# First loads of a linear-attention block from two issuing engines: tile 1 and the keys' weight on ScalarE, the rest of x on SyncE

## The chip, the cores and the metric

One core of one Trainium2 chip runs the whole program. The metric is the device time of one launch in microseconds. The core's engines are TensorE (PE; PEld are its weight loads), VectorE (DVE), ScalarE (ACT), GpSimd (POOL) and SyncE (SP). Each runs its own instructions in the order in which they were issued, and they wait for each other by semaphores. Sixteen DMA engines move data between HBM and SBUF.

## The reference

A pre-norm transformer block on 2048 tokens of width 512, with linear attention of 32 heads (16 wide) and a ReLU feed-forward of width 1792; all inputs are bf16.

```python
def _A_ref(x, wqkv, wo):
    qkv = (x @ wqkv).reshape(B, S, 3, H, Dh) ...      # q, k, v
    phi = lambda t: jnp.where(t > 0, t + 1, jnp.exp(t)) + 1e-6
    pq, pk = phi(q), phi(k)
    kv = jnp.einsum("bhsd,bhse->bhde", pk, v)
    z = jnp.einsum("bhsd->bhd", pk)
    num = jnp.einsum("bhqd,bhde->bhqe", pq, kv)
    den = jnp.einsum("bhqd,bhd->bhq", pq, z)[..., None] + 1e-6
    return (num / den) ... @ wo
h  = x + _A_ref(_layernorm(x), A_wqkv, A_wo)
h2 = h + relu(_layernorm(h) @ B_w1) @ B_w2
```

## The kernel before, in words

**Tiles.** The 2048 tokens are cut into 16 tiles of 128; tile t holds tokens p * 16 + t for partition p. One tile of x is 128 KB: each partition reads one piece of 1 KB from HBM. A load of n neighbouring tiles reads n KB in one piece per partition. The keys' weight (columns 512 to 1023 of `wqkv`) is 512 KB in `wk_sb`, as four blocks of 128 rows; a half is two blocks, 256 KB, in pieces of 1 KB.

**Order.** There is no loop nest. The string `ORDER` lists every step of the kernel by hand, and the last lines of the function call `op_<name>` for each word with its numbers. Since each engine works in issue order, the string sets each engine's own sequence. The words that matter here:

- `lx.t.n` loads n tiles of x from tile t, and `lk.k.n` loads n blocks of the keys' weight from block k; both are issued by SyncE.
- `table` loads ScalarE's function table; `warm.n.b` are TensorE matmuls on zeros that nothing reads.
- `S.t`, `A.t` (VectorE): statistics and mean/variance of tile t. `R.t.n` (ScalarE): reciprocal standard deviation. `N.t` (VectorE): the normalised tile.
- `T.t.b` (TensorE) and `E.t` (ScalarE): transposed tile through PSUM, for tiles 0 to 3. `X.t` (SyncE): the same for later tiles, by a DMA that transposes.
- `K.t.b.k.n` (TensorE): tile t of the keys, n of the four blocks of the product with `wk_sb`. `K.0.3.0.2` needs only blocks 0 and 1, `K.0.3.2.2` blocks 2 and 3.
- `F`, `U` (ScalarE), `M`, `D` (VectorE): phi of the keys: exp, ReLU, minimum, sum. `D.t` writes the features.
- `G.t` (TensorE): the features of tile t times its normalised tile, summed over the 16 tiles.

The first stretch on VectorE is S.0 S.1 A.0 S.2 A.1 S.3 A.2 N.0 A.3 N.1 N.2 N.3 S.4 S.5 A.4 A.5 S.7 N.5 S.6 M.0 A.7 A.6 D.0. On TensorE it is eleven warm-up matmuls, T.0 to T.3, then K.0 (first half), K.1 (first half), K.0 (second half), K.3, K.2 (first half), K.1 (second half), K.2 (second half), G.0, G.3, K.5, K.4. On SyncE it is ten loads (tiles 0, 1, 2, 3, half 0, tiles 4-5, half 1, tiles 6-7, 8-11, 12-15) and then X.5, X.4. ScalarE begins with the table load, then R.0.

Of the kernel before, what the change touches and what calls it, by code (L numbers as in the profile page):

```python
# [15 lines left out]


ORDER = """
const masks table lx.0.1 lx.1.1 lx.2.1 S.0 S.1 A.0 S.2 warm.1.6 lx.3.1 A.1 R.0.1 S.3 A.2 R.1.1 warm.9.6 N.0 A.3
N.1 R.2.1 R.3.1 lk.0.2 N.2 N.3 warm.1.6 T.0.2 T.1.7 lx.4.2 T.2.5 lk.2.2 S.4 E.0 S.5 T.3.4 A.4 K.0.3.0.2 E.1  # L20
K.1.0.0.2 lx.6.2 E.2 E.3 A.5 R.4.2 K.0.3.2.2 S.7 F.0.1 N.5 S.6 K.3.7 M.0.1 lx.8.4 K.2.2.0.2 U.0.1 lx.12.4 A.7
A.6 K.1.0.2.2 D.0.1 F.3.1 U.3.1 R.6.2 N.4 K.2.2.2.2 M.3.1 G.0 D.3.1 G.3 F.2.1 F.1.1 N.6 N.7 S.8 S.9 X.5 X.4
M.2.1 A.8 A.9 U.2.1 U.1.1 K.5.1 R.8.2 K.4.0 M.1.1 D.2.1 F.4.2 D.1.1 N.9 U.4.2 N.8 X.7 S.12 X.6 X.9 G.2 K.7.3
S.13 A.12 A.13 G.1 K.6.2 K.9.1 M.4.2 S.10 R.12.2 F.6.2 N.12 D.4.2 S.11 A.10 U.6.2 X.8 lq.0.2 M.6.2 N.13 G.4 X.12
K.8.0 A.11 R.10.2 D.6.2 lv.0.2 X.13 G.5 G.6 N.10 N.11 S.15 S.14 F.8.2 M.8.2 U.8.2 G.7 X.11 A.15 A.14 D.8.2
R.14.2 N.15 K.12.0 N.14 za.2 za.4 X.10 G.9 lq.2.2 lv.2.2 K.13.1 K.11.3 F.12.2 U.12.2 X.15 X.14 l2.10.4 l2.3.4
l1.0.2 K.10.2 G.8 M.12.2 F.10.2 U.10.2 za.6 D.12.2 M.10.2 za.8 D.10.2 Q.0.0.0 Q.0.1.1 qF.0.0.2 qU.0.0.2 za.10
qM.0.0.2 K.15.3 G.12 K.14.2 F.14.2 G.11 Q.0.2.0 Q.0.3.1 qF.0.2.2 G.13 za.12 M.14.2 W.14.2 zf.12 qD.0.0.2
qM.0.2.2 qU.0.2.2 G.10 G.14 z.3.3.14 G.15 z.1.3.14 z.2.3.14 z.0.3.14 qD.0.2.2 zc Q.1.0.2 gA.0.2 gA.2.2 zh dn.0.1
Q.1.1.3 dnl.0 kv.0.4 kv.2.4 kv.1.4 kv.3.4 lo.0.2 lo.2.2 dnx.0.2.2 qF.1.0.2 dnx.0.0.2 Q.1.2.0 rt.2.7 kx qM.1.0.2  # L30
Q.1.3.1 qF.1.2.2 m.0.4 m.1.5 rv.2 qW.1.0.2 qM.1.2.2 Q.3.1.7 m.3.6 Q.2.3.2 l1.2.2 dt.3 mA.0.2 qW.1.2.2 dt.0 dt.1
m.2.5 Q.2.1.4 dn.1.3 mA.2.2 dm.0.0.2 dm.0.2.2 dnl.1 dnx.1.2.2 Q.2.2.1 h.3.6 dnx.1.0.2 h.1.5 hD.3 dt.7 qF.2.2.2
rt.6.3 s.3 dt.4 re.6 h.0.0 hD.1 qU.2.2.2 dt.5 a.3 hD.0 s.1 s.0 qM.2.2.2 a.0 Q.3.0.6 h.2.5 Q.2.0.3 n.3 n.0 a.1
dm.1.0.2 Q.3.2.0 Q.3.3.1 dm.1.2.2 x.0 x.3 hD.2 n.1 s.2 qF.3.0.2 qU.2.0.2 qF.2.0.2 h.5.2 h.6.3 a.2 qU.3.0.2
qF.3.2.2 qM.2.0.2 h.4.7 n.2 qD.2.0.2 t.2.5 qD.2.2.2 hD.5 hD.4 h.7.4 dn.2.6 hD.7 e.2 dnl.2 x.1 hD.6 qM.3.0.2
p.0.0.5 dnx.2.2.2 p.0.13.7 p.0.1.6 p.0.8.2 p.0.11.4 qD.3.0.2 s.4 dnx.2.0.2 p.0.9.3 l2.7.3 dt.10 pA.0.0.2 dt.11
l2.0.3 dt.9 dt.8 p.0.12.6 qM.3.2.2 qW.3.2.2 s.6 pD.0.12.2 p.0.3.1 p.0.2.0 pA.0.8.2 s.7 r.0.4 dn.3.6 p.0.5.3
p.0.4.2 a.7 dm.2.0.2 dnl.3 pA.0.2.2 dnx.3.0.2 dnx.3.2.2 pA.0.4.2 dm.2.2.2 p.0.7.7 h.9.0 h.8.5 p.0.6.6 n.7 s.5
dt.13 dt.12 p.0.10.3 hD.9 hD.8 s.8 a.6 pD.0.6.2 dt.15 a.4 n.6 dt.14 pA.0.10.2 f.1.1.0.7 dm.3.0.2 dm.3.2.2 h.11.0
f.1.1.7.7 h.12.4 fo.1 s.9 h.15.6 h.14.5 h.10.3 f.0.2.0.7 a.8 a.9 a.5 hD.11 n.5 hD.12 x.6 hD.15 f.3.4.0.7 h.13.7  # L40
f.3.4.7.7 x.7 s.12 n.8 n.4 hD.14 f.0.2.7.7 x.4 x.5 p.1.0.6 f.2.5.0.7 s.11 s.14 hD.13 fo.3 fo.0 hD.10 a.11 s.10
n.9 p.1.5.3 p.1.1.7 s.15 a.12 pA.1.0.2 p.1.4.2 f.2.5.7.7 p.1.13.7 p.1.3.1 a.10 n.12 r.4.4 pA.1.4.2 p.1.2.0 n.11
p.1.8.4 fo.2 a.14 a.15 s.13 p.1.12.6 n.10 p.1.7.2 pD.1.2.2 n.14 p.1.6.1 x.11 p.1.9.5 pA.1.6.2 x.10 a.13 n.15 x.9
x.8 pD.1.8.2 fd.3 f.5.3.0.7 f.7.0.0.7 p.1.10.1 fd.1 fd.0 pA.1.12.2 p.1.11.2 pA.1.10.2 p.2.9.7 p.2.11.6 f.7.0.7.7
p.2.10.5 p.2.5.1 f.5.3.7.7 fo.7 pD.2.10.2 p.2.8.6 p.2.4.0 r.8.4 f.4.4.0.7 f.4.4.7.7 fo.5 p.2.0.2 pD.2.8.2
pD.2.4.2 p.2.1.3 x.12 n.13 p.2.3.6 p.2.2.5 fd.2 f.6.0.0.7 x.14 x.13 pA.2.0.2 pA.2.2.2 x.15 fo.4 p.3.3.7 p.3.7.1
p.3.2.6 p.3.9.5 p.3.8.4 f.6.0.7.7 pD.3.2.2 fo.6 pD.3.8.2 fd.4 p.3.11.7 p.3.4.2 p.3.10.6 p.3.5.3 p.3.6.0
pA.3.10.2 fd.7 pA.3.6.2 p.2.7.7 fd.5 fd.6 p.2.6.6 pA.2.6.2 p.3.13.5 pD.3.4.2 p.3.0.1 p.3.1.2 p.2.13.7 p.2.12.6
f.11.3.0.7 p.3.12.4 pA.3.0.2 pA.2.12.2 r.12.4 pD.3.12.2 f.9.6.0.7 f.14.2.0.7 f.10.7.0.7 f.11.3.7.7 f.10.7.7.7
f.9.6.7.7 f.8.1.0.7 f.12.5.0.7 f.8.1.7.7 f.13.0.0.7 f.15.4.0.14.3.1 f.14.2.7.7 fo.9 fo.10 fo.11 fd.10 fd.11 fd.9  # L50
f.12.5.7.7 fo.8 f.13.0.7.7 f.15.3.0.14.0.2 fd.8 fo.14 fo.12 fo.13 fo.15.3.1 fd.12 f.15.1.0.14.2.1 fd.13
fd.15.3.1 fd.14 fo.15.0.2 fd.15.0.2 fo.15.2.1 fd.15.2.1
"""
# [3 lines left out]
def kernel(  # L57
# [144 lines left out]

    def load_d(dst, src, k, n):
        nc.sync.dma_start(out=dst[:, k : k + n, :], in_=src[:, k : k + n, :])  # L204
# [376 lines left out]
```

## Time and profile before

| | |
|---|---|
| median of 3 runs | 170.55 us (170.41 to 173.28) |
| the profiled execution | 170.57 us |
| its span, first to last instruction | 168.9 us |
| busy: PE / DVE / ACT / POOL | 96% / 60% / 40% / 3% of the span |
| data moved | 15.49 MB, of which the first ten loads 2.5 MB |
| granted TensorE clock | 1.00 |

In a row of the timeline stand the start and the duration in us, engine and line, what is written and read, the count, and in brackets the idle time before it with what ended that. Neighbouring instructions of one kind are merged into one row with their count. DMA issues are listed on SPq (and would be on ACT's queue) with the time that the issue took; the transfer itself lasts longer, and "us to landing" counts from the issue to its last byte.

### The profile page before, as it was taken

To read this page: it belongs to the slowest core of one execution; us is meant where nothing else is said; L and a number is where in the kernel's file an instruction comes from. 1 tells how busy PE (TensorE), PEld (TensorE's weight loads), DVE (VectorE), ACT (ScalarE), POOL (GpSimd) and SP (SyncE) were. 2 spreads that over 40 slices of the span, in tenths; PEclk is the share of its full clock that TensorE was granted. 3 is DMA by queue.
4 is the path that set the end of the run, shared out by engine and by line. 5 is a ranking of instruction groups with operands and counts; after the bars stand their busy time and mean duration, and the time that the engine had idled before them with its cause. 6 is when DMAs were issued, how large, how long until landed. Compare 5 with 4: busy or idle time off the path is not lost.

```text
span 168.9 us, 2311 instructions
## 1 busy us (share of the span) xinstructions
PE 162.5 (96%) x871; PEld 76.1 (45%) x871; DVE 101.1 (60%) x202; ACT 67.7 (40%) x100; POOL 4.7 (3%) x21
## 2 busy tenths in 40 slices
PE   7779999999999999999999999999999999999993
PEld 2333444445554454544444444444444444444552
DVE  3979999997577999776977372047203600204152
ACT  3886784847879865652000504200220245000000
POOL 7300000000000000000000000000000000000000
DMA  5964485999133363534130116300320000002113
GB/s 124 276 240 92 89 178 117 217 385 336 37 64 62 64 157 67 151 62 97 33 64 0 31 36 157 86 4 0 80 76 0 31 4 0 0 0 88 36 35 93
DMA packets 30635, 15.49 MB, mean 92 GB/s; under 512 B 23200, under 2 KB 29600, under 8 KB 30624
## 3 DMA queue, kind: packets, MB, share of 16 engines
q1 hardware_dynamic: 30624, 15.34, 34.9%
q8 instruction: 7, 0.11, 0.3%
q14 instruction: 4, 0.03, 0.1%
HBM read 7.86 MB, written 2.10 MB: 59 GB/s over the span
## 4 chain that ended last, share of the span: by engine, by line
PE 91%; DMA 3%; SPq 2%; DVE 1%; issue 1%
PE bk L530 29%; PE bk L510 29%; PE bk L351 8%; PE bk L307 8%; PE bk L494 8%; PE bk L299 6%; DMA x_nat<-in_A_x_dram 3%; SPq L201 1%; PE bk L448 1%; PE bk L392 1%; SPq L204 1%; PE bk L404 1%; PE bk L270 0%; DVE st L226 0%; DVE pk_lo L327 0%
## 5 line engine op out<-in xcount | busy, mean ns | idle before, releaser
L530 PE MATMUL bk<-w_sb,at 128*128 128x512 bf16 (+2 forms) x252 | 50.7, 355 | 0.0
L510 PE MATMUL bk<-lnT,w_sb 128*128 128x512 bf16 x224 | 50.5, 379 | 0.0
L516 ACT ACTIVATE at<-bk 128x1024 bf16<-128x1024 f32 x17 | 17.3, 1021 | 55.6 <-PE bk L510 55.6
L530 PEld LDWEIGHTS <-at 128*128 128x128 bf16 x252 | 23.6, 98 | 25.2 <-DVE at L521 0.2
L510 PEld LDWEIGHTS <-w_sb 128*128 128x128 bf16 x224 | 21.8, 98 | 26.0
L538 DVE SCALAR_TENSOR_TENSOR gT<-bk,rstd,h_nat 128x512 bf16<-128x512 f32 (+2 forms) x18 | 12.2, 690 | 31.2 <-PE bk L530 31.2
L521 DVE TENSOR_SCALAR at<-bk 128x1024 bf16<-128x1024 f32 x11 | 13.3, 1220 | 20.7 <-PE bk L510 20.4
L317 ACT ACTIVATE eb<-bk 128x1024 bf16<-128x1024 f32 (+1 forms) x18 | 16.6, 926 | 6.7 <-PE bk L299 4.0
L307 PE MATMUL bk<-lnT,wq_sb 128*128 128x512 bf16 x64 | 15.8, 379 | 0.0
L299 PE MATMUL bk<-wk_sb,lnT 128*128 128x512 bf16 x64 | 15.3, 379 | 0.0
L494 PE MATMUL bk<-m_sb,pqs 128*128 128x512 bf16 x64 | 15.3, 379 | 0.0
L351 PE MATMUL bk<-at,h_nat 128*128 128x512 bf16 x56 | 13.6, 379 | 0.0
L320 ACT ACTIVATE rb<-bk 128x1024 bf16<-128x1024 f32 (+1 forms) x14 | 12.5, 903 | 0.7 <-PE bk L307 0.7
L226 DVE BATCH_NORM_STATS2 st<-x_nat 128x6 f32<-128x512 bf16 x16 | 10.5, 684 | 3.0 <-DMA x_nat<-in_A_x_dram 3.0
L500 DVE TENSOR_TENSOR h_nat<-bk,x_nat 128x512 bf16<-128x512 f32 x16 | 10.6, 681 | 2.4 <-PE bk L494 2.3
L228 DVE BATCH_NORM_STATS2 st<-h_nat 128x6 f32<-128x512 bf16 x16 | 10.8, 685 | 0.1
L351 PEld LDWEIGHTS <-h_nat 128*128 128x128 bf16 x64 | 6.2, 97 | 8.8 <-issue 1.8
L299 PEld LDWEIGHTS <-lnT 128*128 128x128 bf16 x64 | 5.9, 98 | 7.8 <-DMA lnT<-h_nat 1.4
L494 PEld LDWEIGHTS <-pqs 128*128 128x128 bf16 x64 | 6.1, 98 | 7.2 <-DVE pqs L484 0.8
L307 PEld LDWEIGHTS <-wq_sb 128*128 128x128 bf16 x64 | 5.9, 97 | 6.5 <-DMA wq_sb<-in_A_wqkv_dram 0.4
L461 ACT ACTIVATE wk_sb<-ld 128x1024 bf16<-128x1024 f32 x8 | 8.1, 1051 | 0.1
L324 DVE TENSOR_SCALAR eb<-eb 128x1024 bf16<-128x1024 bf16 (+1 forms) x18 | 6.9, 383 | 0.6 <-ACT eb L317 0.6
(61 smaller groups left out, 89.0 us busy)
## 6 DMA issues: line engine op xcount, KB each, us to landing
out_dram<-gT SPq DMA_DIRECT2D x15, 128.0 KB, 1.9
w_sb<-in_B_w_dram SPq DMA_DIRECT2D x2, 896.0 KB, 8.4
x_nat<-in_A_x_dram SPq DMA_DIRECT2D x2, 512.0 KB, 7.0
w_sb<-in_B_w_dram SPq DMA_DIRECT2D x2, 512.0 KB, 4.8
w_sb<-in_B_w_dram SPq DMA_DIRECT2D x2, 384.0 KB, 3.5
x_nat<-in_A_x_dram SPq DMA_DIRECT2D x4, 128.0 KB, 2.5
wk_sb<-in_A_wqkv_dram SPq DMA_DIRECT2D x2, 256.0 KB, 4.2
x_nat<-in_A_x_dram SPq DMA_DIRECT2D x2, 256.0 KB, 5.0
```

What stands on the lines that cost most here:

```text
L228: op_s = lambda t: nc.vector.bn_stats(out=st2[:, t, :], in_=h_nat[:, t, :])
L299: nc.tensor.matmul(bk[:, b, :], lhsT=lnT[c][:, kd, j * P : (j + 1) * P], rhs=wk_sb[:, kd, :], start=(kd == 0), stop=(kd == KD - 1),)
L307: nc.tensor.matmul(bk[:, b, :], lhsT=wq_sb[:, kd, j * P : (j + 1) * P], rhs=lnT[c][:, kd, :], start=(kd == 0), stop=(kd == KD - 1),)
L317: nc.scalar.activation(out=buf(eb, kind, i, n), in_=bank(at_bank[kind, i], n), func=ACT.Exp)
L320: nc.scalar.activation(out=buf(rb, kind, i, n), in_=bank(at_bank[kind, i], n), func=ACT.Relu)
L351: nc.tensor.matmul(bk[:, KD + kd, :], lhsT=ln_nat[:, t, kd * P : (kd + 1) * P], rhs=pk(t)[:, 0, :], start=(t == 0), stop=(t == NT - 1),)
L494: nc.tensor.matmul(bk[:, b, :], lhsT=pqs[:, (c * KD + jb) % NQ, j * P : (j + 1) * P], rhs=m_sb[:, jb, :], start=(jb == 0), stop=(jb == KD ...
L510: nc.tensor.matmul(bk[:, b, cols], lhsT=w1_sb[:, kd, f * P : (f + 1) * P], rhs=lnT[c][:, kd, cols], start=(kd == 0), stop=(kd == KD - 1),)
L516: nc.scalar.activation(out=acts[c % 2][:, f : f + n, :], in_=bank(at_bank["p", c, f], n), func=ACT.Relu)
L521: nc.vector.tensor_scalar(out=acts[c % 2][:, f : f + n, :], in0=bank(at_bank["p", c, f], n), scalar1=0.0, scalar2=None, op0=ALU.max,)
L530: nc.tensor.matmul(bk[:, b, 0 : w * P], lhsT=acts[c % 2][:, f, j * P : (j + 1) * P], rhs=w2_sb[:, f, k * P : (k + w) * P], start=(f == 0), ...
L538: nc.vector.scalar_tensor_tensor(out=o_t[:, t % NO, cols], in0=bk[:, at_bank["f", t, k], 0 : w * P], scalar=rstd2[:, t : t + 1], in1=h_nat ...
```

## The change

Two steps are added, `xa` and `la`, which issue the loads of x and of the keys' weight from ScalarE. `xa.1.1 la.0.2 la.2.2` come ahead of `table` in the order, so they are ScalarE's first three instructions. SyncE issues tile 0, tiles 2 and 3 in one transfer, 4-5, 6-7, 8-11 and 12-15, all ahead of the first S. The words `lx.1.1`, `lx.2.1`, `lx.3.1`, `lk.0.2` and `lk.2.2` are gone, and the later `lx` words are moved forward. All other words stand in the old sequence, though the lines of the string break elsewhere.

```diff
 ORDER = """
-const masks table lx.0.1 lx.1.1 lx.2.1 S.0 S.1 A.0 S.2 warm.1.6 lx.3.1 A.1 R.0.1 S.3 A.2 R.1.1 warm.9.6 N.0 A.3
-N.1 R.2.1 R.3.1 lk.0.2 N.2 N.3 warm.1.6 T.0.2 T.1.7 lx.4.2 T.2.5 lk.2.2 S.4 E.0 S.5 T.3.4 A.4 K.0.3.0.2 E.1
-K.1.0.0.2 lx.6.2 E.2 E.3 A.5 R.4.2 K.0.3.2.2 S.7 F.0.1 N.5 S.6 K.3.7 M.0.1 lx.8.4 K.2.2.0.2 U.0.1 lx.12.4 A.7
...
+const masks xa.1.1 la.0.2 la.2.2 table lx.0.1 lx.2.2 lx.4.2 lx.6.2 lx.8.4 lx.12.4 S.0 S.1 A.0 S.2 warm.1.6 A.1
+R.0.1 S.3 A.2 R.1.1 warm.9.6 N.0 A.3 N.1 R.2.1 R.3.1 N.2 N.3 warm.1.6 T.0.2 T.1.7 T.2.5 S.4 E.0 S.5 T.3.4 A.4
+K.0.3.0.2 E.1 K.1.0.0.2 E.2 E.3 A.5 R.4.2 K.0.3.2.2 S.7 F.0.1 N.5 S.6 K.3.7 M.0.1 K.2.2.0.2 U.0.1 A.7 A.6
...
+    def op_xa(t, n):
+        nc.scalar.dma_start(out=x_nat[:, t : t + n, :], in_=x_v[:, t : t + n, :])
+
+    def op_la(k, n):
+        nc.scalar.dma_start(out=wk_sb[:, k : k + n, :], in_=wqkv_v[:, k : k + n, D : 2 * D])
```

More of the change, by code (lines that the diff above doesn't have):

```diff
@@ L18 @@
 ORDER = """
-const masks table lx.0.1 lx.1.1 lx.2.1 S.0 S.1 A.0 S.2 warm.1.6 lx.3.1 A.1 R.0.1 S.3 A.2 R.1.1 warm.9.6 N.0 A.3
-N.1 R.2.1 R.3.1 lk.0.2 N.2 N.3 warm.1.6 T.0.2 T.1.7 lx.4.2 T.2.5 lk.2.2 S.4 E.0 S.5 T.3.4 A.4 K.0.3.0.2 E.1
-K.1.0.0.2 lx.6.2 E.2 E.3 A.5 R.4.2 K.0.3.2.2 S.7 F.0.1 N.5 S.6 K.3.7 M.0.1 lx.8.4 K.2.2.0.2 U.0.1 lx.12.4 A.7
-A.6 K.1.0.2.2 D.0.1 F.3.1 U.3.1 R.6.2 N.4 K.2.2.2.2 M.3.1 G.0 D.3.1 G.3 F.2.1 F.1.1 N.6 N.7 S.8 S.9 X.5 X.4
-M.2.1 A.8 A.9 U.2.1 U.1.1 K.5.1 R.8.2 K.4.0 M.1.1 D.2.1 F.4.2 D.1.1 N.9 U.4.2 N.8 X.7 S.12 X.6 X.9 G.2 K.7.3
@@ L24 @@
[L24 to L48, printed above, removed]
@@ L49 @@
-f.11.3.0.7 p.3.12.4 pA.3.0.2 pA.2.12.2 r.12.4 pD.3.12.2 f.9.6.0.7 f.14.2.0.7 f.10.7.0.7 f.11.3.7.7 f.10.7.7.7
-f.9.6.7.7 f.8.1.0.7 f.12.5.0.7 f.8.1.7.7 f.13.0.0.7 f.15.4.0.14.3.1 f.14.2.7.7 fo.9 fo.10 fo.11 fd.10 fd.11 fd.9
+const masks xa.1.1 la.0.2 la.2.2 table lx.0.1 lx.2.2 lx.4.2 lx.6.2 lx.8.4 lx.12.4 S.0 S.1 A.0 S.2 warm.1.6 A.1
+R.0.1 S.3 A.2 R.1.1 warm.9.6 N.0 A.3 N.1 R.2.1 R.3.1 N.2 N.3 warm.1.6 T.0.2 T.1.7 T.2.5 S.4 E.0 S.5 T.3.4 A.4
+K.0.3.0.2 E.1 K.1.0.0.2 E.2 E.3 A.5 R.4.2 K.0.3.2.2 S.7 F.0.1 N.5 S.6 K.3.7 M.0.1 K.2.2.0.2 U.0.1 A.7 A.6
@@ new lines @@
+K.1.0.2.2 D.0.1 F.3.1 U.3.1 R.6.2 N.4 K.2.2.2.2 M.3.1 G.0 D.3.1 G.3 F.2.1 F.1.1 N.6 N.7 S.8 S.9 X.5 X.4 M.2.1
+A.8 A.9 U.2.1 U.1.1 K.5.1 R.8.2 K.4.0 M.1.1 D.2.1 F.4.2 D.1.1 N.9 U.4.2 N.8 X.7 S.12 X.6 X.9 G.2 K.7.3 S.13 A.12
+A.13 G.1 K.6.2 K.9.1 M.4.2 S.10 R.12.2 F.6.2 N.12 D.4.2 S.11 A.10 U.6.2 X.8 lq.0.2 M.6.2 N.13 G.4 X.12 K.8.0
+A.11 R.10.2 D.6.2 lv.0.2 X.13 G.5 G.6 N.10 N.11 S.15 S.14 F.8.2 M.8.2 U.8.2 G.7 X.11 A.15 A.14 D.8.2 R.14.2 N.15
+K.12.0 N.14 za.2 za.4 X.10 G.9 lq.2.2 lv.2.2 K.13.1 K.11.3 F.12.2 U.12.2 X.15 X.14 l2.10.4 l2.3.4 l1.0.2 K.10.2
@@ new lines @@
+G.8 M.12.2 F.10.2 U.10.2 za.6 D.12.2 M.10.2 za.8 D.10.2 Q.0.0.0 Q.0.1.1 qF.0.0.2 qU.0.0.2 za.10 qM.0.0.2 K.15.3
+G.12 K.14.2 F.14.2 G.11 Q.0.2.0 Q.0.3.1 qF.0.2.2 G.13 za.12 M.14.2 W.14.2 zf.12 qD.0.0.2 qM.0.2.2 qU.0.2.2 G.10
+G.14 z.3.3.14 G.15 z.1.3.14 z.2.3.14 z.0.3.14 qD.0.2.2 zc Q.1.0.2 gA.0.2 gA.2.2 zh dn.0.1 Q.1.1.3 dnl.0 kv.0.4
+kv.2.4 kv.1.4 kv.3.4 lo.0.2 lo.2.2 dnx.0.2.2 qF.1.0.2 dnx.0.0.2 Q.1.2.0 rt.2.7 kx qM.1.0.2 Q.1.3.1 qF.1.2.2
+m.0.4 m.1.5 rv.2 qW.1.0.2 qM.1.2.2 Q.3.1.7 m.3.6 Q.2.3.2 l1.2.2 dt.3 mA.0.2 qW.1.2.2 dt.0 dt.1 m.2.5 Q.2.1.4
@@ new lines @@
+dn.1.3 mA.2.2 dm.0.0.2 dm.0.2.2 dnl.1 dnx.1.2.2 Q.2.2.1 h.3.6 dnx.1.0.2 h.1.5 hD.3 dt.7 qF.2.2.2 rt.6.3 s.3 dt.4
+re.6 h.0.0 hD.1 qU.2.2.2 dt.5 a.3 hD.0 s.1 s.0 qM.2.2.2 a.0 Q.3.0.6 h.2.5 Q.2.0.3 n.3 n.0 a.1 dm.1.0.2 Q.3.2.0
+Q.3.3.1 dm.1.2.2 x.0 x.3 hD.2 n.1 s.2 qF.3.0.2 qU.2.0.2 qF.2.0.2 h.5.2 h.6.3 a.2 qU.3.0.2 qF.3.2.2 qM.2.0.2
+h.4.7 n.2 qD.2.0.2 t.2.5 qD.2.2.2 hD.5 hD.4 h.7.4 dn.2.6 hD.7 e.2 dnl.2 x.1 hD.6 qM.3.0.2 p.0.0.5 dnx.2.2.2
+p.0.13.7 p.0.1.6 p.0.8.2 p.0.11.4 qD.3.0.2 s.4 dnx.2.0.2 p.0.9.3 l2.7.3 dt.10 pA.0.0.2 dt.11 l2.0.3 dt.9 dt.8
@@ new lines @@
+p.0.12.6 qM.3.2.2 qW.3.2.2 s.6 pD.0.12.2 p.0.3.1 p.0.2.0 pA.0.8.2 s.7 r.0.4 dn.3.6 p.0.5.3 p.0.4.2 a.7 dm.2.0.2
+dnl.3 pA.0.2.2 dnx.3.0.2 dnx.3.2.2 pA.0.4.2 dm.2.2.2 p.0.7.7 h.9.0 h.8.5 p.0.6.6 n.7 s.5 dt.13 dt.12 p.0.10.3
+hD.9 hD.8 s.8 a.6 pD.0.6.2 dt.15 a.4 n.6 dt.14 pA.0.10.2 f.1.1.0.7 dm.3.0.2 dm.3.2.2 h.11.0 f.1.1.7.7 h.12.4
+fo.1 s.9 h.15.6 h.14.5 h.10.3 f.0.2.0.7 a.8 a.9 a.5 hD.11 n.5 hD.12 x.6 hD.15 f.3.4.0.7 h.13.7 f.3.4.7.7 x.7
+s.12 n.8 n.4 hD.14 f.0.2.7.7 x.4 x.5 p.1.0.6 f.2.5.0.7 s.11 s.14 hD.13 fo.3 fo.0 hD.10 a.11 s.10 n.9 p.1.5.3
@@ new lines @@
+p.1.1.7 s.15 a.12 pA.1.0.2 p.1.4.2 f.2.5.7.7 p.1.13.7 p.1.3.1 a.10 n.12 r.4.4 pA.1.4.2 p.1.2.0 n.11 p.1.8.4 fo.2
+a.14 a.15 s.13 p.1.12.6 n.10 p.1.7.2 pD.1.2.2 n.14 p.1.6.1 x.11 p.1.9.5 pA.1.6.2 x.10 a.13 n.15 x.9 x.8 pD.1.8.2
+fd.3 f.5.3.0.7 f.7.0.0.7 p.1.10.1 fd.1 fd.0 pA.1.12.2 p.1.11.2 pA.1.10.2 p.2.9.7 p.2.11.6 f.7.0.7.7 p.2.10.5
+p.2.5.1 f.5.3.7.7 fo.7 pD.2.10.2 p.2.8.6 p.2.4.0 r.8.4 f.4.4.0.7 f.4.4.7.7 fo.5 p.2.0.2 pD.2.8.2 pD.2.4.2
+p.2.1.3 x.12 n.13 p.2.3.6 p.2.2.5 fd.2 f.6.0.0.7 x.14 x.13 pA.2.0.2 pA.2.2.2 x.15 fo.4 p.3.3.7 p.3.7.1 p.3.2.6
@@ L51 @@
+p.3.9.5 p.3.8.4 f.6.0.7.7 pD.3.2.2 fo.6 pD.3.8.2 fd.4 p.3.11.7 p.3.4.2 p.3.10.6 p.3.5.3 p.3.6.0 pA.3.10.2 fd.7
+pA.3.6.2 p.2.7.7 fd.5 fd.6 p.2.6.6 pA.2.6.2 p.3.13.5 pD.3.4.2 p.3.0.1 p.3.1.2 p.2.13.7 p.2.12.6 f.11.3.0.7
+p.3.12.4 pA.3.0.2 pA.2.12.2 r.12.4 pD.3.12.2 f.9.6.0.7 f.14.2.0.7 f.10.7.0.7 f.11.3.7.7 f.10.7.7.7 f.9.6.7.7
+f.8.1.0.7 f.12.5.0.7 f.8.1.7.7 f.13.0.0.7 f.15.4.0.14.3.1 f.14.2.7.7 fo.9 fo.10 fo.11 fd.10 fd.11 fd.9
 f.12.5.7.7 fo.8 f.13.0.7.7 f.15.3.0.14.0.2 fd.8 fo.14 fo.12 fo.13 fo.15.3.1 fd.12 f.15.1.0.14.2.1 fd.13
```

## Prediction

> **What bounds the kernel now.** I read the page first: busy time, then the chain that ended last.
>
> ```profile
> span 168.9 us, 2311 instructions
> PE 162.5 (96%) x871; PEld 76.1 (45%) x871; DVE 101.1 (60%) x202; ACT 67.7 (40%) x100; POOL 4.7 (3%) x21
> DMA packets 30635, 15.49 MB, mean 92 GB/s; under 512 B 23200, under 2 KB 29600, under 8 KB 30624
> PE 91%; DMA 3%; SPq 2%; DVE 1%; issue 1%
> ```
>
> TensorE is 96% busy and 91% of the chain. The change touches only first loads, so the question is where the other 9% lies. The chain in order of time and the stage view place it (columns of the last two rows: stretch; length, then busy time and instruction count of PE, PEld, DVE, ACT, POOL).
>
> ```profile
> 4.12 5.80 DMA x_nat<-in_A_x_dram
> 9.98 0.57 issue
> 11.86 0.44 DVE pk_lo L327
> 12.33 1.02 PE bk L351 x4
> 26.77 2.59 PE bk L299 x12
> 143.29 22.75 PE bk L530 x133
> 12.33:30.23 17.90, 17.86 (x81) 7.68 (x81) 17.45 (x44) 12.46 (x22) 0.00 (x0) 1.00 0.61 131
> 30.23:166.00 135.77, 135.77 (x748) 64.64 (x746) 74.96 (x132) 47.40 (x59) 0.00 (x0) 1.00 0.29 76
> ```
>
> From 12.33 us TensorE never pauses again until 166, so the time is the moment of G.0 (the first L351 matmul, 12.33) plus a constant, and whatever the change does must show as a shift of that moment. One cushion lies behind it: 80 matmuls between 12.33 and 30.23 at the undisturbed pace 2.59/12 = 0.216 us would take 17.3 us of the 17.9, so up to 0.6 us of a late start can be caught up there, if the other engines keep their times.
>
> What leads to 12.33 is in the timeline (start, duration, engine, line).
>
> ```profile
> 0.79 1.28 ACT L166 ACT_TABLE_LOAD   x1 [0.79 <-PEq L565]
> 1.25 3.91 PE L215 MATMUL bk<-m_sb 128*128 128x512 bf16 x11 [1.25 <-DVE ones L177]
> 3.08 1.30 DVE L226 BATCH_NORM_STATS2 st<-x_nat 128x6 f32<-128x512 bf16 x2 [1.86 <-DMA x_nat<-in_A_x_dram]
> 4.39 0.66 DVE L226 BATCH_NORM_STATS2 st<-x_nat 128x6 f32<-128x512 bf16 x1
> 4.50 0.29 ACT L232 ACTIVATE rstd<-mv,eps 128x1 f32<-128x1 f32 x1 [2.43 <-DVE mv L227]
> 4.83 0.20 ACT L233 ACTIVATE rstd<-rstd 128x1 f32<-128x1 f32 x1
> 5.16 0.69 DVE L226 BATCH_NORM_STATS2 st<-x_nat 128x6 f32<-128x512 bf16 x1
> 5.85 0.45 DVE L251 TENSOR_SCALAR h_nat<-x_nat,mv,rstd 128x512 bf16<-128x512 bf16 x1
> 6.36 1.49 PE L270 MATMUL bk<-ident,h_nat 128*128 128x128 bf16 x16 [1.20 <-DVE h_nat L251]
> 7.69 3.62 PE L299 MATMUL bk<-wk_sb,lnT 128*128 128x512 bf16 x16
> 8.51 0.30 DVE L227 BATCH_NORM_AGGREGATE mv<-st 128x2 f32<-128x6 f32 x2
> 9.28 0.58 ACT L317 ACTIVATE eb<-bk 128x512 bf16<-128x512 f32 x1
> 9.95 0.69 DVE L226 BATCH_NORM_STATS2 st<-x_nat 128x6 f32<-128x512 bf16 x1 [1.14 <-DMA x_nat<-in_A_x_dram]
> 11.86 0.43 DVE L327 TENSOR_TENSOR pk_lo<-rb,eb 128x512 bf16<-128x512 bf16 x1
> 12.33 1.02 PE L351 MATMUL bk<-pk_lo,h_nat 128*128 128x512 bf16 x4 [1.03 <-DVE pk_lo L327]
> ```
>
> Two paths meet at G.0. **The vector path:** VectorE stands still for 1.14 us until tiles 6 and 7 have landed (S.7 at 9.95); S.7, N.5, S.6, M.0 are queued ahead of D.0 (11.86), which releases G.0. **The TensorE path:** S.0 (3.08), S.2 (4.39), S.3 (5.16), N.0 (5.85), transposes (6.36), then 16 matmuls with the keys' weight, 7.69 to 11.31. That path arrives 1.03 us early. So a gain is at most 1.03 us, and a front that slips by less than about 1.0 us costs nothing.
>
> **When each load lands.** The DMA view of each issue's own window gives size and time to landing; the queue's issues stand beside them.
>
> ```profile
> 0.80 0.40 SPq L201
> 4.12 1.42 SPq L201 DMA_DIRECT2D x_nat<-in_A_x_dram  x3
> x_nat<-in_A_x_dram SPq DMA_DIRECT2D x1, 128.0 KB, 2.3
> x_nat<-in_A_x_dram SPq DMA_DIRECT2D x1, 128.0 KB, 2.4
> x_nat<-in_A_x_dram SPq DMA_DIRECT2D x1, 128.0 KB, 2.9
> wk_sb<-in_A_wqkv_dram SPq DMA_DIRECT2D x1, 256.0 KB, 3.9
> x_nat<-in_A_x_dram SPq DMA_DIRECT2D x1, 256.0 KB, 4.1
> wk_sb<-in_A_wqkv_dram SPq DMA_DIRECT2D x1, 256.0 KB, 4.6
> x_nat<-in_A_x_dram SPq DMA_DIRECT2D x1, 256.0 KB, 5.8
> x_nat<-in_A_x_dram SPq DMA_DIRECT2D x1, 512.0 KB, 6.6
> 2.19 0.43 SPq L201
> 3.14 0.47 SPq L201
> 3.65 0.43 SPq L204
> ```
>
> The eight landings are those of tile 0, tile 1, tile 3, weight half 0, tiles 4-5, weight half 1, tiles 6-7 and tiles 8-11. An issue takes 0.47 us with its gap ((4.12 - 0.80)/7), so they start at 0.80, 1.26, 2.19, 2.66, 3.14, 3.65, 4.12 and 4.6. Adding gives a curve of KB landed: 128 at 3.1, 256 at 3.7, 512 at 5.1, 768 at 6.6, 1024 at 7.2, 1280 at 8.25, 1536 at 9.9, 2048 at 11.2. Tile 0 needs 2.3 us alone; tiles 6-7 need 5.8, so 3.5 us of that is waiting behind earlier bytes. Issue time is little of it. Rows of 2 KB go faster: 256 KB of 1 KB rows (tiles 1 to 3) took 5.1 - 3.7 = 1.4 us, 256 KB of 2 KB rows (tiles 4-5) 7.2 - 6.6 = 0.7.
>
> **The change part by part.**
>
> **ScalarE's three issues.** The trace has no issue by ScalarE. Nearest row: SyncE's at 0.43 to 0.47; the bound below is nothing, the one above the 1.28 of the table load. At 0.47 they take 1.4 us, the table load runs from 2.2 to 3.5, and R.0 is first needed at 4.50: hidden with 1.0 us to spare. If they took 1.28 each, the load would end at 5.9 and R.0 (0.5 us of work) at 6.4 against N.0 at 5.85: 0.6 us late, still inside the 1.03. I take nothing.
>
> **SyncE's queue.** Ten issues become six, so it is free 1.9 us sooner. The next thing in it, X.5, waits for N.5, which VectorE has behind S.7 (9.95), and not for the queue: nothing.
>
> **The bytes now come from two queues.** This is the step that decides, and the trace of before, with one load queue, doesn't show how two share the 16 engines. The bounds are "in turn, whole transfers, nearly the old order" and "packet by packet". The page counts 1,024 packets of 2 KB to 8 KB and thousands of 1 KB, one per row of a partition, so a row is the unit that moves, and I take packet by packet as the likelier. Then, by the curve:
>
> 1. Tile 0 shares with tile 1: up to 256 KB ahead, landing by 3.7 instead of 3.1. This does not add to the next point.
> 2. Tiles 2-3 (2 KB rows) finish when half of weight half 0 (1 KB rows) has gone as well: 128 + 128 + 256 + 128 = 640 KB, on the curve 5.8, less half of the 0.75 us that the 2 KB rows save: 5.4. S.2 waited till 4.39, and now for both tiles: 1.0 us late; S.3 had 0.1 us to spare (S.2 ended at 5.05), so N.0 and everything to K.0 slips 0.9. Bounds: 0 (landing at 4.4) to 1.4 (5.8).
> 3. Tiles 6-7 land after 1408 KB, near 9.1. But A.5 now ends at 8.81 + 0.9 = 9.7, so VectorE no longer waits for them; S.7 is at 9.7. This gain, 0.25 us, would show only if TensorE's path were earlier.
> 4. Weight half 1 is last in ScalarE's queue: its 40 rows per engine alternate with 40 rows of SyncE's (8 of 1 KB, 24 of 2 KB, 8 of 4 KB), so 2048 KB have gone by then: 11.2 on the curve, less the 0.75: 10.5. Before it landed at 8.25. Bounds: 8.25 and 11.2.
> 5. K.0's second half is the fifth of the 16 matmuls: it stood at 7.69 + 4 x 3.62/16 = 8.6, and slips with the front to 9.5. It now waits until 10.5; behind it in TensorE's queue stand the other K matmuls and G.0, and ScalarE's F.0 (9.28) waits for K.0. Twelve matmuls at 0.226 end at 13.2: **G.0 slips from 12.33 to 13.2, +0.9 us.** F.0 and D.0 follow K.0 and are done by about 12.6, earlier.
> 6. The cushion of 0.6 us takes some back, because transposes by DMA that TensorE waited for are not later by as much (VectorE is not behind): I take 0.4.
>
> Sum: +0.9 - 0.4 = +0.5 us. The profiled execution took 170.57 us, 1.7 around its span of 168.9; the median of the runs is 170.55, the same. Forecast **171.1 us**. By step 4's bounds its own range is 170.4 (half 1 at 8.25: G.0 at 11.31 + 0.9 = 12.2, -0.1) to 172.2 (half 1 at 11.2: G.0 at 13.9, +1.6).
>
> [...]
>
> **The rivals.**
>
> **Served in turn (faster).** Whole transfers alternate: tiles 0, 1, 2-3, half 0, 4-5, half 1, 6-7. Order and bytes are the old ones. Tiles 2-3 land at 5.1 - 0.4 = 4.7: front +0.3, TensorE's path arrives at 11.6. Half 1 is back near 8.25, before its use at 8.9. Tiles 6-7 lose the 0.75 us: 9.2, S.7 0.7 sooner, G.0 by the vector path at 11.7: -0.6, and the cushion takes a little: 170.1 us (169.6, the whole 1.03, to 170.6). For it: the curve is set by bytes and not by issue. Against: the one-row packets. Should the two issuers hold each other up as they issue, the issues alternate too, and this case holds.
>
> **ScalarE's queue starts late (slower).** If tile 1 comes as late as though the table load ran first (1.28 us), S.1 is at 4.9, the front slips 1.2, past the 1.03 that decides, and half 1 comes 1.28 later than whatever its share: 11.8 at most, G.0 at 14.5 at most; a middle value is +1.5, less 0.4: 171.7. Against it: both engines were ready at 0.79 and 0.80.
>
> **TensorE's clock falls.** The pause between the warm-up matmuls (end 5.16) and the transposes grows from 1.20 to about 2.1 us. The eleven warm-up matmuls took 3.91 us, 0.36 each on the mean, against 0.226 in the K stage. If the clock fell, 16 K matmuls would cost at least 0.13 more each, 2.1 us, and up to double, 3.6: 2.9 in the middle, and with the 0.5 above 174.0. After the pauses of 1.20 and 1.03 the stage rows have the clock at 1.00, so nothing speaks for it but the longer pause. [...]
>
> **Chances.** Packet by packet 0.50, in turn 0.32, late queue 0.13, clock 0.05. The time is the first one's, 171.1. The range runs from 169.8 (most of the in-turn case) to 172.2 (the upper bound of step 4, with the late queue inside it). A measurement of this kernel tells about 2% from no change, 3.4 us: no case gains that (the most is 1.03), so faster 0.01; only the clock passes it upwards, in part: slower 0.03; the rest, 0.96, is no change.
>
> **What would show it.** Right: S.0 at 3.3 to 3.7, S.2 near 5.4, S.7 with no wait for x, a pause of about 1 us inside the 16 K matmuls whose releaser is the weight's transfer, G.0 near 13.2, TensorE unbroken after it. Step 4 is wrong if half 1 lands before 9.5: G.0 then comes at 12.2 or sooner and the time is at or under 170.5. Step 2 is wrong if S.2 stays near 4.4. The whole is wrong if TensorE pauses after G.0, or if the clock is below 1.00.

## Result, and the profile after

The changed kernel takes 171.22 us (median of 16 runs, 170.39 to 171.94), the kernel before 170.55 (16 runs beside it): a ratio of 1.005, interval 1.0027 to 1.0072. It is slower by 0.7 us, clear of zero and far inside the 2% that counts as no change. The forecast was 171.1 us in a range of 169.8 to 172.2. The number was right, but the step that carried it was not: most of the time went to a mechanism that the prediction held at 0.05.

The timeline of the changed kernel, rows answering to those of before (line numbers are 6 higher behind the new functions: L305 is K, L357 is G):

```profile
0.79 0.41 ACTq L207 DMA_DIRECT2D x_nat<-in_A_x_dram  x1
1.23 0.98 ACTq L210 DMA_DIRECT2D wk_sb<-in_A_wqkv_dram  x2
1.25 4.48 PE L221 MATMUL bk<-m_sb 128*128 128x512 bf16 x11 [1.25 <-DVE ones L177]
2.25 1.28 ACT L166 ACT_TABLE_LOAD   x1 [2.25 <-issue]
3.86 1.29 DVE L232 BATCH_NORM_STATS2 st<-x_nat 128x6 f32<-128x512 bf16 x2 [2.64 <-DMA x_nat<-in_A_x_dram]
5.26 0.30 ACT L238 ACTIVATE rstd<-mv,eps 128x1 f32<-128x1 f32 x1 [1.73 <-DVE mv L233]
5.71 0.70 DVE L232 BATCH_NORM_STATS2 st<-x_nat 128x6 f32<-128x512 bf16 x1 [0.49 <-DMA x_nat<-in_A_x_dram]
7.06 0.38 DVE L257 TENSOR_SCALAR h_nat<-x_nat,mv,rstd 128x512 bf16<-128x512 bf16 x1
7.50 1.74 PE L276 MATMUL bk<-ident,h_nat 128*128 128x128 bf16 x16 [1.78 <-DVE h_nat L257]
9.04 5.10 PE L305 MATMUL bk<-wk_sb,lnT 128*128 128x512 bf16 x16
9.91 0.66 DVE L232 BATCH_NORM_STATS2 st<-x_nat 128x6 f32<-128x512 bf16 x1
12.96 0.43 DVE L333 TENSOR_TENSOR pk_lo<-rb,eb 128x512 bf16<-128x512 bf16 x1
13.97 1.03 PE L357 MATMUL bk<-pk_lo,h_nat 128*128 128x512 bf16 x4
```

S.0 is 0.8 us later than before (3.86 against 3.08), S.2 1.3 (5.71 against 4.39), K.0 1.35 (9.04 against 7.69). S.7 no longer waits for tiles 6 and 7. The 16 K matmuls then take 5.10 us instead of 3.62, and no row of that stretch waits for the weight. G.0 comes at 13.97 instead of 12.33. The stage view says why (length; busy time and count of PE, PEld, DVE, ACT, POOL; then the granted clock, the DMA share and GB/s):

```profile
5.20:8.62 3.42, 1.64 (x15) 0.69 (x13) 2.92 (x11) 2.37 (x10) 0.86 (x3) 1.00 1.06 407
8.50:8.60 0.10, 0.10 (x3) 0.00 (x0) 0.10 (x2) 0.10 (x2) 0.00 (x0) 1.00 0.91 369
8.60:8.70 0.10, 0.08 (x2) 0.07 (x2) 0.10 (x1) 0.10 (x2) 0.00 (x0) 0.58 1.02 410
8.60:12.00 3.40, 3.38 (x12) 1.46 (x12) 2.98 (x7) 2.08 (x7) 0.00 (x0) 0.50 0.32 129
12.00:12.10 0.10, 0.10 (x2) 0.07 (x1) 0.00 (x0) 0.10 (x1) 0.00 (x0) 0.85 0.00 0
```

**TensorE's clock fell to half** at 8.6 us and stayed there for 3.4 us, over the first half of the K stage's matmuls. The 5.10 us are 1.5 more than 3.62. The clock records of this trace step at 5.20 (up to full), 8.62 (down) and 12.03 (up), each 3.41 us after the last. In the 3.4 us before the fall TensorE was busy for 1.64 us (the row 5.20:8.62). The column reads 1.00 before the first record too, where it can't be trusted: the warm-up matmuls from 1.64 to 5.06 us start 0.43 us apart, twice the 0.216 of the K stage before. Of 16 runs, seven show a granted clock of 0.99 over the span and nine show 1.00: the seven have a median of 171.55 us (171.35 to 171.94), the nine 170.73 (170.39 to 171.40). So the added 0.7 us of the median is a mix: about 0.2 us in every run, and another 0.8 in nearly half.

The weight was early, not late. The DMA view of the issues (ScalarE's half 0, then, from the windows of the next issues, half 1 and tiles 6-7):

```profile
wk_sb<-in_A_wqkv_dram ACTq DMA_DIRECT2D x1, 256.0 KB, 5.0
wk_sb<-in_A_wqkv_dram ACTq DMA_DIRECT2D x1, 256.0 KB, 5.9
x_nat<-in_A_x_dram SPq DMA_DIRECT2D x1, 256.0 KB, 6.1
```

Half 0 landed at 1.23 + 5.0 = 6.2, half 1 at 1.7 + 5.9 = 7.6 (before 8.25), tiles 6-7 at 2.2 + 6.1 = 8.3 (before 9.9).

### The profile page after: what moved, and what is told of

The parts are those of the page before. It is cut to its first block, busy times and chain, and to the rows that moved or that the text cites. A ratio compares the mean times of both kernels' runs of the same rounds, so it can differ in the third digit from the quotient of the medians.

```text
span 169.9 us, 2310 instructions
## 1 busy us (share of the span) xinstructions
PE 164.1 (97%) x871; PEld 77.2 (45%) x871; DVE 101.4 (60%) x202; ACT 67.8 (40%) x100; POOL 4.8 (3%) x21
## 4 chain that ended last, share of the span: by engine, by line
PE 94%; DMA 3%; DVE 1%; SPq 0%; issue 0%
PE bk L536 29%; PE bk L516 28%; PE bk L305 9%; PE bk L313 8%; PE bk L357 8%; PE bk L500 8%; DMA x_nat<-in_A_x_dram 3%; PE bk L276 1%; PE bk L454 1%; DVE st L232 1%; PE bk L398 1%; PE bk L410 1%; SPq L201 0%; PE bk L376 0%; DVE gT L544 0%; DVE h_nat L257 0%
## 5 line engine op out<-in xcount | busy, mean ns | idle before, releaser
L305 PE MATMUL bk<-wk_sb,lnT 128*128 128x512 bf16 x64 | 16.8, 407 | 0.0
L357 PE MATMUL bk<-at,h_nat 128*128 128x512 bf16 x56 | 13.7, 379 | 0.0
L326 ACT ACTIVATE rb<-bk 128x1024 bf16<-128x1024 f32 (+1 forms) x14 | 12.5, 901 | 0.7 <-PE bk L313 0.7
L232 DVE BATCH_NORM_STATS2 st<-x_nat 128x6 f32<-128x512 bf16 x16 | 10.5, 681 | 3.1 <-DMA x_nat<-in_A_x_dram 3.1
L305 PEld LDWEIGHTS <-lnT 128*128 128x128 bf16 x64 | 6.6, 104 | 8.5 <-issue 1.9
L357 PEld LDWEIGHTS <-h_nat 128*128 128x128 bf16 x64 | 6.2, 98 | 7.3
```

The costliest lines, as they stand in the source:

```text
L232: op_S = lambda t: nc.vector.bn_stats(out=st[:, t, :], in_=x_nat[:, t, :])
L305: nc.tensor.matmul(bk[:, b, :], lhsT=lnT[c][:, kd, j * P : (j + 1) * P], rhs=wk_sb[:, kd, :], start=(kd == 0), stop=(kd == KD - 1),)
L326: nc.scalar.activation(out=buf(rb, kind, i, n), in_=bank(at_bank[kind, i], n), func=ACT.Relu)
L357: nc.tensor.matmul(bk[:, KD + kd, :], lhsT=ln_nat[:, t, kd * P : (kd + 1) * P], rhs=pk(t)[:, 0, :], start=(t == 0), stop=(t == NT - 1),)
```

## The experiments

Two theories stood against each other. **Clock:** the late first tiles leave TensorE with too little to do between warm-up and K stage, the clock falls in some runs, and this is most of the loss. **Front delay:** the late tiles themselves move G.0, whatever the clock. Beside it stood the question why two queues make the first tiles late. All ratios are against runs of the kernel before on the same chip.

### More warm-up in the changed kernel

```diff
-warm.9.6
+warm.13.6
```

> The changed kernel with four more warm-up matmuls on zeros (15 in place of 11), whose result nothing reads. Clock theory: the added time is TensorE at half clock in the K stage, after a pause of 1.8 us behind the warm-up. With four more (0.22 to 0.43 us each) the pause shrinks to under 0.9 us, no run shows a clock below 1.00, spans gather at 168.6 to 169.0 and the median falls from 171.2 to 170.2 - 170.6. Rival, front delay: the tiles that land late cost the time, the clock only goes with it; then G.0 stays later than 12.33 and the median stays within 0.3 us of 171.2.

Measured: 170.72 us (12 runs), ratio 1.0019 (0.9994 to 1.0044). All twelve runs have a clock of 1.00. The timeline of its first matmuls:

```profile
1.25 4.92 PE L221 MATMUL bk<-m_sb 128*128 128x512 bf16 x15 [1.25 <-DVE ones L177]
7.62 1.53 PE L276 MATMUL bk<-ident,h_nat 128*128 128x128 bf16 x16 [1.45 <-DVE h_nat L257]
9.00 3.62 PE L305 MATMUL bk<-wk_sb,lnT 128*128 128x512 bf16 x16
12.51 1.02 PE L357 MATMUL bk<-pk_lo,h_nat 128*128 128x512 bf16 x4
```

The tiles are as late as in the changed kernel (K.0 at 9.00 against 9.04), yet the K stage takes 3.62 us again and G.0 is at 12.51. The median is that of the nine runs of the changed kernel with a clock of 1.00, 170.73. Together with the two groups of runs this shows the clock to be the larger part of the loss. Two expectations were missed: the pause shrank only to 1.45 us, not under 0.9, and the median is above 170.2 to 170.6, since G.0 is still 0.2 us later than before.

### The same warm-up in the kernel before

```diff
-warm.9.6
+warm.13.6
```

> Control: the kernel before with the same four more warm-up matmuls. Clock theory: its pause of 1.2 us was short enough, so nothing is gained, ratio 0.998 to 1.002 (it could lose up to 0.5 us if the four matmuls push the transposes). Rival, that a longer warm-up helps any order of loads: it gains 0.5 us or more here too.

Measured: 170.33 us, ratio 1.0004 (0.9979 to 1.0030). A longer warm-up was worth nothing here, where the first tiles are early, as the clock theory expected.

### A shorter warm-up in the kernel before

```diff
-warm.9.6
+warm.6.6
```

> The kernel before with three fewer warm-up matmuls (8 in place of 11), loads untouched. Clock theory: the pause ahead of the transposes grows from 1.2 to about 1.8 us, as in the changed kernel, and a part of the runs, a quarter to three quarters, shows a clock of 0.99 with a span about 1 us longer; median 170.6 to 171.3. Rival, that the low clock belongs to the loads and not to the pause: all runs at 1.00 and 170.2 to 170.6.

Measured: 170.83 us, ratio 1.0017 (0.9988 to 1.0046). The pause grew to 1.64 us, but only one run of twelve has a clock of 0.99 (171.13 us). The median lies in its expected range, but the expectation of a quarter to three quarters of the runs failed. So the length of the pause alone does not decide.

```profile
1.25 3.59 PE L215 MATMUL bk<-m_sb 128*128 128x512 bf16 x8 [1.25 <-DVE ones L177]
6.48 1.53 PE L270 MATMUL bk<-ident,h_nat 128*128 128x128 bf16 x16 [1.64 <-DVE h_nat L251]
7.85 3.62 PE L299 MATMUL bk<-wk_sb,lnT 128*128 128x512 bf16 x16
```

The time from the end of the warm-up to the first K matmul, with the short transposes in it, orders these three better: 2.8 us in the changed kernel with 15 warm-ups (0 of 12 runs low), 3.0 here (1 of 12), 3.3 in the changed kernel (7 of 16). It is an ordering of single profiles with an exception below (2.2 us, 2 of 12, all loads on SyncE).

The traces say more. In the first 20 us the clock fell in five profiles, each time for about 3.4 us: in the changed kernel from 8.62 to 12.03 us, with tiles 2 and 3 apart from about 9.1 to 12.5, with tile 1 alone from about 7.3 to 10.7, with the second queue late from about 16.1 to 19.5 and with the weight held back from about 13.4 to 16.8 (kernels below). The second and the third are estimates from the clock of the window rows (0.98 over 8.90:9.10 and 0.74 over 12.40:12.60; 0.76 over 6.00:8.50 and 0.82 over 10.00:12.00), the last two from the weight loads that start 0.43 us apart there in place of 0.216. In the 3.4 us before the fall TensorE was busy for 1.64 us in the changed kernel and, by the timelines, for an estimated 1.0 to 1.7 in the other four. But with the weight held back TensorE stood still from 8.20 to 10.79 us, busy for only 0.8 us of the 3.4 before 10.79, and with the second queue late it stood still for 3.52 us up to 15.06; the four matmuls straight behind took 1.02 us in both, the full pace, and the fall came 1.0 to 2.6 us later. So little work goes with the falls, but neither its amount nor the pause is shown to set them. No experiment varied this alone, and the condition itself stays open.

### Tiles 2 and 3 in two transfers again

```diff
-lx.0.1 lx.2.2 lx.4.2
+lx.0.1 lx.2.1 lx.3.1 lx.4.2
```

> The changed kernel with tiles 2 and 3 in two transfers on SyncE again; the rest stays. Front-delay theory: S.2 waited for both tiles (5.71); with tile 2 alone it starts near 5.1, N.0 0.3 to 0.6 us sooner, the pause of TensorE falls from 1.8 to about 1.3 us, and the share of runs with the lower clock falls from half to under a quarter: median 170.5 to 170.9. Rival, sharing of the engines by the two queues delays the first tiles whatever their cut: S.0 stays at 3.9, S.2 at 5.4 or later, median 171.0 to 171.4.

Measured: 171.65 us, ratio 1.0075 (1.0045 to 1.0105), and five of six runs at 0.99. S.0 came at 4.30, S.2 at 5.59, N.0 at 7.21. So the merging of tiles 2 and 3 alone is not what made the front late in the changed kernel. The rival holds in kind (S.0 is even later), though the median lies above its 171.0 to 171.4.

### Only the weight on ScalarE

```diff
-xa.1.1 la.0.2 la.2.2 table lx.0.1 lx.2.2 lx.4.2
+table la.0.2 la.2.2 lx.0.1 lx.1.1 lx.2.1 lx.3.1 lx.4.2
```

> ScalarE issues only the two weight halves, after its table load; tiles 0 to 3 go one by one on SyncE, then 4-5, 6-7, 8-11, 12-15. Sharing theory: the first two tiles have the engines to themselves, S.0 at 3.1 and S.1 at 3.7 as before, S.2 by 4.6, the pause back to 1.2 to 1.5 us, clock 1.00. Tiles 6-7 land near 8.5 in place of 9.9, S.7 no longer waits, and G.0 comes at 11.6 to 11.9 in place of 12.33: median 169.9 to 170.3, faster than both. Rival, that nothing before 12.33 is worth anything because the stage behind it takes it back: 170.4 to 170.7.

Measured: 171.57 us, ratio 1.0074 (1.0045 to 1.0102): a miss. The table load did not hold back the issues behind it, as the timeline of ScalarE and the queue shares between 2.5 and 4.5 us show (queue q10 is ScalarE's, q1 SyncE's; packets, MB, share of the engines):

```profile
0.80 1.28 ACT L166 ACT_TABLE_LOAD   x1 [0.80 <-PEq L571]
0.83 0.97 ACTq L210 DMA_DIRECT2D wk_sb<-in_A_wqkv_dram  x2
q10 hardware_dynamic: 494, 0.48, 71.1%
q1 hardware_dynamic: 208, 0.18, 30.0%
```

So the weight left with tile 0 and took 71% of the engines exactly while tiles 1 to 3 were wanted. Tile 1 landed 3.4 us after its issue instead of 2.4. Tile 0 itself was not late: S.0 came at 3.47, and over the profiles in which ScalarE issued no load before 3 us it came at 3.07 to 3.47.

This profile has a granted clock of 1.00, yet its transposes and first K matmuls ran slowly (1.49 and 3.62 us before):

```profile
7.56 1.89 PE L276 MATMUL bk<-ident,h_nat 128*128 128x128 bf16 x16 [1.44 <-DVE h_nat L257]
9.24 4.15 PE L305 MATMUL bk<-wk_sb,lnT 128*128 128x512 bf16 x16
```

Its eleven warm-up matmuls took 4.88 us, 0.43 us from start to start throughout, and in 9.50:10.00 only two K matmuls are at work, where before it was four (8.00:8.50). An estimate from the 0.53 us that the K stage took longer is that its first two or three matmuls ran so, to about 10.3 us. So by the pace the clock had not fallen here; it had not yet risen (the transposes took the same 1.89 us with tile 1 alone at a clock of 0.50). A run listed at 1.00 can hide this, so the counts of runs at 0.99 in this document are the least that were slowed.

### Tile 1 alone on ScalarE

```diff
-const masks table lx.0.1 lx.1.1 lx.2.1
+const masks xa.1.1 table lx.0.1 lx.2.1
```

> The kernel before, but tile 1 is issued by ScalarE as its first instruction; tiles 2 and 3 apart and the weight stay on SyncE in the old order. Sharing theory: tile 0 shares with tile 1 only (S.0 at 3.4 to 3.7), S.2 and S.3 stay within 0.3 us of before since no byte is ahead of them that was not before; time within 0.2 us of before, 170.2 to 170.6. Rival, that any first use of a second queue costs: S.0 at 3.9 and median 170.9 or more.

Measured: 171.02 us, ratio 1.0028 (1.0003 to 1.0053), five of twelve runs at 0.99. In its profile both first transfers, of 128 KB each, needed over 3 us, and S.0 started at 4.26:

```profile
x_nat<-in_A_x_dram ACTq DMA_DIRECT2D x1, 128.0 KB, 3.3
x_nat<-in_A_x_dram SPq DMA_DIRECT2D x1, 128.0 KB, 3.4
```

The rival holds: a single tile on the second queue already costs the front, 1.2 us against before (0.8 against the latest S.0 named above) where equal sharing of 256 KB allowed 0.6. That any first use costs tile 0 is not shown, since with only the weight there S.0 was in time. Both first tiles come late instead of one early and one late, and VectorE's work on tile 0 loses its head start.

### The same loads, all on SyncE, with and without the longer warm-up

```diff
-xa.1.1 la.0.2 la.2.2 table lx.0.1 lx.2.2 lx.4.2 lx.6.2 lx.8.4
+table lx.0.1 lx.1.1 lx.2.2 lk.0.2 lx.4.2 lk.2.2 lx.6.2 lx.8.4
```

> No load on ScalarE: SyncE issues tile 0, tile 1, tiles 2-3 in one, half 0, tiles 4-5, half 1, tiles 6-7, 8-11, 12-15 back to back, the mix of the changed kernel in one queue. Sharing theory: without a second queue the first tiles have the engines to themselves again: S.0 at 3.1 to 3.4, S.2 by 5.1, pause of TensorE 1.2 to 1.5 us, clock 1.00 in all runs, and the later bytes flow slower, under 350 GB/s between 6 and 8.5 us where the changed kernel had 399 to 426; median 170.2 to 170.6. Rival, that the merged tiles 2-3 alone cost the front: S.2 at 5.4 or later and the low clock in some runs, median 170.9 or more.

> The all-on-SyncE order (tiles 2-3 in one transfer, all loads back to back) with 15 warm-up matmuls. Clock theory: the two low-clock runs in twelve disappear, median 170.1 to 170.4. G.0 again near 11.8, and the wait for transposed tiles behind it again near 1.9 us in total against 1.4 before, so no more than 0.2 us of the 0.5 gained at G.0 is left at the end. Rival, that the earlier G.0 is kept: 169.8 to 170.0.

Measured: 170.47 us, ratio 1.0016 (0.9990 to 1.0041), two of twelve runs at 0.99; with 15 warm-ups 170.45 us, ratio 0.9983 (0.9960 to 1.0006), none of twelve. The expected clock of 1.00 in all runs of the first was missed. Back in one queue, tile 0 is early again (S.0 at 3.21) and most of the lost time is gone. The front is not all back: S.2 came at 5.13, waiting for the merged tiles 2-3, and K.0 at 8.29, 0.6 us later than before (8.68 and 1.0 us with 15 warm-ups). So 0.6 to 1.0 of the 1.35 us by which K.0 slipped in the changed kernel appears without a second queue as well, and the rival, that the merged tiles cost the front, holds in part. In the first of the two G.0 came at 11.80, 0.5 us before the kernel before, but its span is 168.9 us all the same. The waits of TensorE and of its weight loads show where that went (engine and line, releaser: us in total, times, longest):

```profile
8.29 3.62 PE L305 MATMUL bk<-wk_sb,lnT 128*128 128x512 bf16 x16
11.80 1.02 PE L357 MATMUL bk<-pk_lo,h_nat 128*128 128x512 bf16 x4
PE bk L305 <- DMA lnT<-h_nat: 0.6, 1, 0.6
PEld L305 <- DMA lnT<-h_nat: 1.9, 3, 1.0
```

Before, the weight loads' wait was 1.4 us in four times, and TensorE itself had none. In this profile TensorE stood 0.6 us for a tile that a DMA transposes, which is about what G.0 had gained. With the longer warm-up G.0 was at 12.19, not near 11.8, because S.2 waited till 5.53 in that profile.

### Second queue late: tiles 6-7 after R.0

```diff
-xa.1.1 la.0.2 la.2.2 table lx.0.1 lx.2.2 lx.4.2 lx.6.2 lx.8.4 lx.12.4
+table lx.0.1 lx.1.1 lx.2.1 lx.3.1 lk.0.2 lx.4.2 lk.2.2 lx.8.4 lx.12.4
-R.0.1 S.3
+R.0.1 xa.6.2 S.3
```

> Order of the kernel before on SyncE, but tiles 6-7 are issued by ScalarE after R.0, near 5.0 us, when tiles 0 to 3 have landed. Sharing theory: the front stays (S.0 3.1 to 3.4, N.0 near 5.9), the second queue only shares with the weight and tiles 4-5, tiles 6-7 land at 8.0 to 9.0 in place of 9.9, S.7 at 8.8 to 9.2, G.0 at 11.4 to 11.8: median 169.6 to 170.0. Rival, that the half 1 of the weight or tiles 4-5 pay for it, or that the stage behind takes it back: 170.3 to 170.8.

Measured: 174.02 us, ratio 1.0158 (1.0105 to 1.0211): far off. Tiles 6-7 were issued at 5.20 and landed 7.5 us later. Between 5.2 and 8.6 us the trace has no packet of q10 at all, though between 6.5 and 7.0 us the engines were busy for only two to five tenths of the time:

```profile
5.20 0.37 ACTq L207 DMA_DIRECT2D x_nat<-in_A_x_dram  x1
x_nat<-in_A_x_dram ACTq DMA_DIRECT2D x1, 256.0 KB, 7.5
q1 hardware_dynamic: 520, 0.84, 76.9%
12.68 0.69 DVE L232 BATCH_NORM_STATS2 st<-x_nat 128x6 f32<-128x512 bf16 x1 [3.63 <-DMA x_nat<-in_A_x_dram]
```

### The weight held back behind tiles 0 to 3

```diff
+    def op_hold():
+        nc.scalar.activation(out=nmean[:, 0:1], in_=mask[:, 0:1], func=ACT.Copy)
-xa.1.1 la.0.2 la.2.2 table lx.0.1 lx.2.2 lx.4.2
+table hold la.0.2 la.2.2 lx.0.1 lx.1.1 lx.2.1 lx.3.1 lx.4.2
-warm.9.6
+warm.13.6
```

> ScalarE issues the two weight halves, but only after a small copy of one column of a mask that GpSimd finishes near 2.35 us, so after SyncE's issues of tiles 0 to 3 (0.80 to 2.6 us); SyncE goes on with tiles 4-5, 6-7 and the rest; 15 warm-up matmuls. Theory that transfers are served in the order of their issue, whichever engine issues: tiles 0 to 3 have the engines first, S.0 at 3.1 to 3.5, N.0 at 5.9 to 6.3, half 1 by 8.0, tiles 6-7 by 8.7, S.7 no longer waits, G.0 at 11.4 to 11.8, clock 1.00. Rival, packet by packet: a half in flight takes its share from tiles 2 and 3, S.2 at 5.0 or later. What follows: if the stage behind keeps the gain, median 169.6 to 170.0; if the transposes by DMA give it back, 170.2 to 170.5.

Measured: 174.23 us, ratio 1.0192 (1.0138 to 1.0247). The front was as early as hoped (S.0 at 3.07, N.0 at 5.83), but the weight, issued at 3.07 and 3.6, landed 7.7 and 9.5 us later, and K.0 stood still for it, first 2.6 and then 1.4 us. Between 8.0 and 9.5 us the queues shared as follows:

```profile
q1 hardware_dynamic: 139, 0.49, 82.0%
q10 hardware_dynamic: 104, 0.10, 18.5%
10.79 1.02 PE L308 MATMUL bk<-wk_sb,lnT 128*128 128x512 bf16 x4 [2.59 <-DMA wk_sb<-in_A_wqkv_dram]
13.23 4.44 PE L308 MATMUL bk<-wk_sb,lnT 128*128 128x512 bf16 x12 [1.42 <-DMA wk_sb<-in_A_wqkv_dram]
```

In this stretch packets are nearly even (104 to 139), bytes one to five, since SyncE's rows were of 2 and 4 KB by then. The theory of service in the order of issue failed. A stall like the one that the prediction described appears here, in another kernel.

## Why the prediction was right or wrong

**The frame held in the main.** In the changed kernel no pause of TensorE follows G.0. The time is not G.0 plus a constant: G.0 slipped by 1.64 us and the span grew by 1.0, and with all loads on SyncE an earlier G.0 (11.80) gave the same span.

**Steps 1 to 3, the front: right in kind, too small.** S.0 was said to come by 3.7 and came at 3.86; S.2 5.4 and 5.71; S.7 without a wait at 9.7 and 9.91. The slip of K.0 was put at 0.9 and measured 1.35. That the second queue delays tile 0 is shown by the kernel that leaves the merging away (late all the same) and by the one without the second queue (early again). Of K.0's slip of 1.35 us, 0.6 to 1.0 stays in one queue, where S.2 waits for the merged tiles 2-3 (5.13 and 5.53). Alone, this delay costs little: the runs of the changed kernel with a clock of 1.00 take 170.73, 0.2 us over before. That the TensorE path had 1.03 us to spare was read rightly.

**Steps 4 and 5, the weight's second half: wrong.** It was to land at 10.5 and hold up TensorE; it landed at 7.6, below its lower bound of 8.25, and no K matmul waited for it. In place of the +0.9 us that it gave the sum at G.0, the run with 15 warm-ups and a clock of 1.00 shows 0.2 (12.51), from the front. The step that failed is the choice of "packet by packet" for this arrangement, with the old landing curve set under it. The landings follow the issues instead (tiles 0 and 1, tiles 2-3, half 0, tiles 4-5, half 1, tiles 6-7). The rival "in turn" had that order, but its whole transfers are not seen: between 4.5 and 7 us both queues moved packets, and nearly the same bytes.

```profile
q10 hardware_dynamic: 460, 0.44, 52.3%
q1 hardware_dynamic: 263, 0.48, 50.3%
```

From 6 us on, too, bytes flowed faster than before (399 to 426 GB/s against 262 to 350). That rival's front, S.2 near 4.7, was not seen, so its gain did not come either.

**The rival "clock falls": this is what happened.** A clock below 1.00 was also its own sign that the whole is wrong. It was given 0.05, and 174.0 us with 2.1 to 3.6 us added to the K stage; seven of 16 runs show it, and it cost 1.5 us in the K stage of the profile and 0.8 at the end. Two readings misled. The clock of 1.00 after pauses of 1.20 and 1.03 us was taken to speak for one of 2.1 as well. And the price let the whole stage run slow until its end, where the clock was back after 3.4 us. Its lower figure, 0.13 us for a matmul, came from the mean of a warm-up that itself changes pace, from 0.43 to 0.22 us. Its upper figure, double, is the pace of matmuls at a clock of 0.50 (0.43 against 0.216 us), but for seven of the 16 matmuls only. And the clock fell in this trace behind a pause of 1.78 us, shorter than the 2.1 foreseen.

**Step 6, the cushion: right.** I took 0.4 us. G.0 to the first L307 was 17.90 us before; after it is 13.97 to 31.41, 17.44:

```profile
31.41 1.73 PE bk L313 x8
```

So 0.46 us was caught up. The 171.1 was thus luck: a stall that did not happen was priced about as high as a slow clock that did, and the median lies between two groups of runs.

**ScalarE's issues and SyncE's queue:** nothing, as said. The issues took 0.41 to 0.49 us, the table load ended at 3.5, R.0 came at 5.26.

## What to carry to other kernels

Before moving first loads to a second issuer, ask which load is wanted first and what its neighbours take from it: here S.0 came 0.8 us later (0.4 later than in the latest profile with one queue at the start), and the earlier landing of the later loads gave nothing back, because G.0 waited for the work on the first tiles. A delay that the schedule hid still cost through the clock here, where TensorE idled between its warm-up and its first long stage (0.8 us in seven of 16 runs), and four more dummy matmuls took that cost away (none of 12 runs at 0.99). And look at the clock run by run: a median between two groups has no mechanism of its own.
